# Attention and expert kernel on one core: four early loads issued by ScalarE, and the order planned with other numbers

## The chip, the cores and the metric

The kernel runs on one core of one Trainium2 chip. The metric is the device time of one execution in microseconds (us), the median of several runs.

## The reference

The reference is attention with rotary positions, followed by a two-layer expert with a leaky activation. Batch 4, 8 heads, sequence 576, head size 64; model width 512, hidden width 2048.

```python
q_rot, k_rot = (rotate(q), rotate(k))          # x1*cos - x2*sin, x1*sin + x2*cos
scores = scale * np.matmul(q_rot, k_rot.transpose(0, 1, 3, 2))
scores = scores - np.max(scores, axis=-1, keepdims=True)
attn = np.exp(scores)
attn = attn / (np.sum(attn, axis=-1, keepdims=True) + 1e-09)
out = np.matmul(attn, v)                        # (4, 8, 576, 64) -> x: (2304, 512)
h = x @ w_in
g = np.maximum(h, 0.0) + alpha * np.minimum(h, 0.0)
y = g @ w_out
```

All inputs are f32; w_in and w_out come as the words of 8-byte values, which VectorE puts together as f32.

## The kernel before

**Tiles and blocks.** The 2304 rows are 18 tiles of 128 rows, two to a block, so 9 blocks. A tile's attention goes by pairs of heads: queries and keys are loaded with a half-turned copy beside them, multiplied with the table of cosines and sines (`q_mul` L725, `k_mul` L516), and the two halves are added (`q_add` L733, `k_add` L525). TensorE makes the scores of two heads (L777), VectorE the maximum of each row (`mx`, L830), ScalarE the exponential and its sum (`exp`, L834).

**Two ways through.** In tiles 0 and 1 the exponentials stay in f32: TensorE turns them (`f_turn`, L874), ScalarE or VectorE copies them to SBUF (`f_copy`, L883 and L884), and TensorE multiplies with V (`f_pv`, L878). From tile 2 on they are split into a high and a low 16-bit part (`p_hi`, `p_lo`), a DMA transpose issued by SP turns them (`p_turn`, L851, tile `pt`), and TensorE multiplies (`pv`, L858). The experts are the same in f32 for blocks 0 and 1 (L945, L974) and in split 16-bit parts for the others (L951, L992). Weights come from DRAM into `wraw` buffers (L620); VectorE puts them together (L602, L607, L611), ScalarE takes their bound (L635, L645).

**What sets the order.** The program first writes a list of operations with their reads, writes and the engines that could run each. A planner (class `Plan`) then plays the list through, and each engine's instructions are issued in the order that it finds. For every engine that is free, it takes the waiting operation with the lowest due time. A due time is the operation's place (`at`, in units of 1/16 of a block) plus a number from the table `OFF`, by name and block or batch; the second engine that could run it adds a number from `PEN`. An operation with two possible engines goes to the one that is free and comes to it first. A load is planned on SP with 450 ns of issue, 1050 ns of delay and its size at 400 bytes per ns, behind the transfers planned before it; a DMA transpose has 1310 and 70 ns. For TensorE the planner keeps a book on the clock: every operation fills time with a weight `full`, and durations double while the book says that the clock is low. So every number in the tables can change the order on all engines, and none changes what is computed.

**The start.** On SP stand the two halves of the table (`tab`), `alpha`, tile 0's queries in two loads (`q_load`), the unit matrix (`eye`), and pair 0's and pair 1's keys in two loads each (`k_load`), then tile 1's queries and the values. All of these go through the helper `load`, L462 and L463. With `LEADS[0] = 3.15`, block 0's first pair has the place -19.15; a next pair of block 0 lies 2 later, tile 1's first pair 8 later. `tab` has -100, `alpha` -60, `eye` -59.

```python
keys:    load("k_load", b, at, r, ...)          # at: place of the pair
queries: load("q_load", t, at, raw, ...)        # at: place of the tile's first pair
run:     at = o.at + off(o.name, o.ph) + (pen(o.name, o.ph) if n else 0.0)
```

Of the kernel before, what the change touches and what calls it, by code (L numbers as in the profile page):

```python
# [45 lines left out]
    "a_bound": [13.39],  # L46
    "alpha": [4.11],
    "beta": [19.29],
    "eps": [-20.32],
    "exp": [-203.03, -13.08, -31.0, 7.42, -20.79, -6.72, -8.0, 2.63, 7.03],  # L50
    "eye": [20.48],
    "f_copy": [12.93],
    "f_pv": [14.63],
    "f_turn": [59.59],
    "gh": [-119.2, -119.2, -0.01, 27.77, -4.93, -6.46, 15.98, 77.17, 37.16],
    "gl": [329.17, 329.17, 3.75, 117.32, 59.74, -18.86, 34.4, 47.73, 66.05],
    "k_add": [15.8, -47.1, -62.28, 47.21],
# [12 lines left out]
    "pv": [-4.69, 13.78, 4.19, 3.85, 52.85, 0.63, -24.67, -14.01, 3.0],  # L70
    "q_add": [-9.89, -9.05, -13.47, -3.57, 13.4, 64.02, 22.21, -52.45, 79.61, 5.48, 28.34, 41.15, 10.07, 17.29, 0.89, 43.95, -3.57, 12.45],
    "q_hi": [126.19, 126.19, 126.19, 126.19, 126.19, -40.04, 20.21, -64.76, 17.73, 12.18, 7.82, 14.08, 21.0, -80.01, 13.39, -11.81, -24.61, -2.03],
    "q_lo": [-274.45, -274.45, -274.45, -274.45, -274.45, -5.86, -46.35, 2.77, 2.98, -5.57, 6.91, 31.12, 81.93, 51.48, -30.41, 5.61, -53.97, 18.63],
    "q_load": [-36.37, 13.88, -35.2, 9.7, -28.6, -11.73, -8.87, -103.41, 2.72, 9.37, -12.59, -11.1, -4.78, -14.91, -14.97, -8.7, -22.17, -23.39],
    "q_mul": [0.2, 30.31, 38.86, 32.22, 23.45, -6.9, 11.63, 40.42, 35.74, 16.54, 5.05, -21.77, -62.23, -14.81, -8.77, -21.73, 11.08, 110.02],
    "qd_hi": [151.43, 151.43, 82.32, 188.91, 235.61, 196.33, 29.99],
    "qd_lo": [8.59, 8.59, 20.78, -28.98, 85.57, 37.05, 4.13],
    "qd_zero": [-26.0, -26.0, 14.21, 88.92, 81.33, 26.3, 1.39],
    "relu": [-62.53, -48.77, -15.14, -35.39, -40.71, -80.66, -6.1, -1.65, 59.45],
    "res": [-79.62, -68.8, -29.62, -71.23, 62.15, 37.72, -40.93, -1.3, -1.64],  # L80
    "scores": [-34.62, 18.22, -3.17, -1.13, 2.75, 2.96, -29.27, -29.27, -0.88],
    "store": [-23.0, -149.27, -35.86, 55.49, 23.16, -23.49, 20.05, 10.42, -13.25],
    "tab": [-72.81, -3.78],
    "v_bound": [-8.18, 13.64, 68.86, -0.72],
    "v_hi": [0.49, -14.0, 43.8, 56.91],
# [16 lines left out]
    "wo_load": [55.26, 4.66, 16.03, 31.9],
    "x_hi": [-226.3, -226.3, 1.25, 16.57, -33.84, -50.05, -39.14, -24.72, 30.89],
    "x_lo": [113.28, 113.28, 23.69, -16.73, -45.15, -15.99, -85.91, 51.43, 0.18],
    "x_turn": [-86.07, -86.07, -0.04, 8.63, 97.54, 24.21, -20.71, 45.23, 34.62],
    "xw": [30.4, 30.4, 6.35, -56.71, -60.57, -24.46, -2.94],
    "y": [-35.54, 8.31, 67.96, -16.15, 14.03, -14.1, -10.06, -15.84, -90.05],
    "y_copy": [-2.21, 1.09],
    "y_turn": [42.78, 15.85],
# [1047 lines left out]
```

## Time and profile before

| | |
|---|---|
| median of 3 runs | 639.58 us (638.41 to 640.85) |
| the profiled execution | 643.7 us, span from first to last instruction 641.9 us |
| mean granted TensorE clock | 0.986 |
| VectorE, ScalarE, GpSimd busy | 76%, 56%, 34% of the span |
| the 16 DMA engines busy | 65.4% of the span by the main queue |
| moved | 90.97 MB, mean 142 GB/s |

Shares are of the span. The granted clock is 1.00 at full speed (2.4 GHz) and 0.5 at half (1.2 GHz); a mean over a stretch can lie between them. DMA share is the mean busy share of the 16 DMA engines. Engines in the rows: PE is TensorE's matmul, PEld its weight load, DVE VectorE, ACT ScalarE, POOL GpSimd, SPq the queue of SP.

### The profile page before, as it was taken

The page shows a single profiled execution, that of the slowest core. Times are in us where ns is not written, and L with a number is a line of the kernel's source. Part 1 is how long each engine was busy: PE and PEld are TensorE (multiplying, and loading weights), DVE is VectorE, ACT ScalarE, POOL GpSimd, SP SyncE. Part 2 cuts the span into 40 slices and gives each one's busy share as a digit, 9 for nine tenths or more (in the row PEclk, how much of TensorE's full clock was granted, in tenths as well). Part 3 has the DMA queues.
Part 4 walks back from the last instruction along what each step waited for, and adds up shares of the span by engine and source line. Part 5 has one row for each costly group of instructions (what it writes and reads, how often), then busy time and mean ns, then how long its engine had stood idle before and what let it go on. Part 6 is the DMA issues. An engine that isn't in the chain of part 4 may idle for free.

```text
span 641.9 us, 13987 instructions
## 1 busy us (share of the span) xinstructions
PE 602.4 (94%) x5478; PEld 431.1 (67%) x5478; DVE 485.0 (76%) x800; ACT 360.7 (56%) x808; POOL 218.5 (34%) x178
## 2 busy tenths in 40 slices
PE   1789789999999999999998999999999999999997
PEld 1668656667776767677665777777777667776664
DVE  5797979999999876769986789879985537853332
ACT  1455756555795648547665566767653435733332
POOL 4470300016746516436633343585331101210000
PEclk9878999999999999999999999999999999999999
DMA  8951798958955659759898977976855303752000
GB/s 303 407 178 64 240 275 211 261 79 202 215 130 111 121 88 173 133 92 198 146 187 140 165 145 108 189 129 161 129 111 92 87 1 66 135 103 24 34 1 34
DMA packets 188499, 90.97 MB, mean 142 GB/s; under 512 B 168721, under 2 KB 176529, under 8 KB 188433
## 3 DMA queue, kind: packets, MB, share of 16 engines
q1 hardware_dynamic: 188432, 90.08, 65.4%
q8 instruction: 43, 0.70, 0.5%
q14 instruction: 24, 0.19, 0.1%
HBM read 41.82 MB, written 4.72 MB: 72 GB/s over the span
## 4 chain that ended last, share of the span: by engine, by line
PE 68%; DMA 17%; DVE 9%; ACT 2%; issue 2%; SPq 1%; POOL 0%; DVEq 0%; ACTq 0%; POOLq 0%
PE h L951 20%; PE pair L992 20%; PE pair L777 8%; PE v L858 7%; DMA pt<-pp 7%; PE h L945 5%; DMA wraw<-in_moe_w_in_dram 5%; PE pair L974 4%; DVE mx L830 2%; DMA wraw<-in_moe_w_out_dram 2%; DVE pp L847 1%; PE pair L874 1%; PE v L878 1%; DVE r L968 1%; DMA kraw<-in_k_dram 1%
## 5 line engine op out<-in xcount | busy, mean ns | idle before, releaser
L951 PE MATMUL h<-xt,wi 128*128 128x256 f16 (+1 forms) x1344 | 165.2, 273 | 2.1 <-DVE r L968 1.2
L951 PEld LDWEIGHTS <-wi 128*128 128x128 f16 (+1 forms) x1344 | 129.3, 98 | 37.0 <-issue 5.2
L992 PE MATMUL pair<-wh,gh 128*128 128x512 f16 x448 | 133.4, 379 | 0.3 <-DVE os L470 0.3
L968 DVE SCALAR_TENSOR_TENSOR r<-r,beta,h 128x256 f32<-128x256 f32 x144 | 68.5, 476 | 64.8 <-ACT r L965 63.1
L830 DVE TENSOR_REDUCE mx<-pair 128x1 f32<-128x576 f32 x144 | 103.1, 749 | 12.3 <-PE pair L777 8.7
L965 ACT ACTIVATE r<-h 128x256 f32<-128x256 f32 x144 | 54.7, 380 | 101.0 <-PE h L951 69.8
L834 ACT ACTIVATE e<-pair,mx 128x576 f32<-128x576 f32 x112 | 82.2, 737 | 43.5 <-DVE mx L830 42.7
L985 POOL TENSOR_TENSOR gl<-r,gh 128x256 bf16<-128x256 f32 x57 | 51.1, 897 | 133.4 <-ACT gh L982 116.0
L847 DVE SCALAR_TENSOR_TENSOR pp<-e,pp 128x576 f16<-128x576 f32 x96 | 82.8, 870 | 8.6 <-ACT pp L843 7.6
L858 PEld LDWEIGHTS <-pt 128*128 128x128 f16 (+1 forms) x2016 | 71.6, 101 | 23.8 <-DMA pt<-pp 10.9
L992 PE MATMUL pair<-wh,gl 128*128 128x512 f16 x224 | 84.9, 379 | 0.0
L858 PE MATMUL v<-vv,pt 128*128 128x64 f16 (+1 forms) x2016 | 78.5, 194 | 6.7 <-DMA pt<-pp 6.6
L982 ACT ACTIVATE gh<-r 128x256 f16<-128x256 f32 x106 | 43.7, 414 | 47.8 <-PE pair L992 29.2
L945 PE MATMUL h<-xt,wi 128*128 128x256 f32 x256 | 61.8, 384 | 4.5 <-DVE r L968 3.5
L974 PE MATMUL pair<-wo,r 128*128 128x512 f32 x128 | 61.9, 607 | 0.0
L945 PEld LDWEIGHTS h<-xt,wi 128*128 128x128 f32 x256 | 47.5, 190 | 21.2 <-DVE r L968 7.8
L992 PEld LDWEIGHTS <-gh 128*128 128x128 f16 x448 | 39.9, 98 | 32.1 <-issue 2.1
L777 PE MATMUL pair<-kh,qn 64*128 64x288 f32 x576 | 50.9, 308 | 0.0
L985 DVE TENSOR_TENSOR gl<-r,gh 128x256 bf16<-128x256 f32 x55 | 27.4, 499 | 27.3 <-ACT gh L982 27.2
L777 PEld LDWEIGHTS pair<-kh,qn 64*128 64x128 f32 x576 | 39.7, 184 | 11.0 <-issue 7.8
L843 ACT ACTIVATE pp<-e 128x576 f16<-128x576 f32 x59 | 40.1, 680 | 8.7 <-DMA pt<-pp 7.0
L725 POOL TENSOR_TENSOR qr<-qr,tab 128x1024 f32<-128x1024 f32 (+1 forms) x14 | 29.4, 2106 | 34.6 <-DMA qr<-in_q_dram 34.6
(124 smaller groups left out, 755.5 us busy)
## 6 DMA issues: line engine op xcount, KB each, us to landing
qr<-in_q_dram SPq DMA_DIRECT2D x17, 512.0 KB, 4.8
wraw<-in_moe_w_in_dram SPq DMA_DIRECT2D x16, 512.0 KB, 5.8
wraw<-in_moe_w_out_dram SPq DMA_DIRECT2D x16, 512.0 KB, 6.7
kraw<-in_k_dram SPq DMA_DIRECT2D x12, 576.0 KB, 4.8
out_dram<-os SPq DMA_DIRECT2D x18, 256.0 KB, 2.2
vraw<-in_v_dram SPq DMA_DIRECT2D x12, 320.0 KB, 3.8
kraw<-in_k_dram SPq DMA_DIRECT2D x8, 288.0 KB, 7.1
vv<-vv SPq DMA_DIRECT2D x32, 64.0 KB, 2.5
```

Source lines behind the costliest of these rows:

```text
L777: nc.tensor.matmul(out=ps[h]()[:, x, :HS], lhsT=qn()[r, p] if b == 0 else qn()[r, i, p], rhs=kt()[r, c] if b == 0 else kt()[r, j, c], star ...
L830: lambda e: nc.vector.tensor_reduce(out=mx()[a:z], in_=ps()[a:z, :, :HS], axis=AX.XY, op=ALU.max, negate=True),
L834: lambda e: nc.scalar.activation(out=e_y() if t in IN_PLACE else e_y().rearrange("p (x c) -> p x c", x=2), in_=ps()[a:z, :, :HS], func=ACT ...
L847: lambda e: nc.vector.scalar_tensor_tensor(out=e_z(pp()[a:z, 1]), in0=e_y(), scalar=E_SC, in1=e_z(pp()[a:z, 0]), op0=ALU.mult, op1=ALU.sub ...
L858: nc.tensor.matmul(out=v_b()[c:d, 2 * p + g], lhsT=pt()[:, s, o:o + d - c], rhs=vt()[:, g, w], start=(n == 0), stop=(n == len(order) - 1))
L945: nc.tensor.matmul(out=h_y(), lhsT=w32(kk, j // FG)[:, f], rhs=x()[:, kk], start=(kk == 0), stop=(kk == KC - 1))
L951: nc.tensor.matmul(out=h_y(), lhsT=wt.bitcast(BF16) if w else wt, rhs=xs.bitcast(BF16) if y else xs, start=(kk == 0 and n == 0), stop=(kk ...
L965: lambda e: nc.scalar.activation(out=g(), in_=h_y(), func=ACTF.Relu, scale=-1.0),
L968: lambda e: nc.vector.scalar_tensor_tensor(out=g(), in0=g(), scalar=beta_b()[:, j:j + 1], in1=h_y(), op0=ALU.mult, op1=ALU.add),
L974: nc.tensor.matmul(out=po()[:, x], lhsT=g()[:, x * 128:(x + 1) * 128], rhs=wf[j // 2]()[:, j % 2], start=(j == 0), stop=(j == KF - 1))
L985: lambda e: ENG[e].tensor_tensor(out=gl(), in0=g(), in1=gh(), op=ALU.subtract),
L992: nc.tensor.matmul(out=po()[:, x], lhsT=s()[:, ts], rhs=w, start=(j == 0 and c == 0), stop=(j == KF - 1 and c == 2))
```

## The change

Three things change. First, `load` gets an argument `first`; with it the load is issued by ScalarE and planned with 480 ns on that engine. It is given for tile 0's queries, `alpha` and `eye`. Second, the planner's model: all engines start at 800 ns, a DMA transpose that finds more than 200 ns of transfers queued ahead of it takes 800 ns more of the transfer time, and the weights `full` of five operations in the book on the clock are other numbers. Third, all numbers of `OFF` and `PEN` (some 500) and three constants are new.

```diff
-    "k_add": [15.8, -47.1, -62.28, 47.21],
+    "k_add": [11.07, -14.72, -13.74, 12.24],
-    "k_load": [-0.18, -49.98, -22.1, 11.87],
+    "k_load": [-31.77, -8.33, -4.32, -64.95],
-    "alpha": [4.11],
+    "alpha": [1.56],
-    "eye": [20.48],
+    "eye": [-0.94],
-    "q_load": [-36.37, 13.88, -35.2, 9.7, ...
+    "q_load": [1.15, -28.05, -24.01, 9.81, ...
-    "tab": [-72.81, -3.78],
+    "tab": [-27.28, -23.21],
-    "v_load": [30.89, -20.13, 4.99, 11.68],
+    "v_load": [-9.8, -11.66, -37.11, -9.65],
...
 PEN = {
-    "k_add": [6.07, -5.88, 33.15, -22.07],
+    "k_add": [9.48, -88.82, -8.62, -1.45],
...
-PW, LW, BACKLOG = 174.78, 6.46, 4989.5
+PW, LW, BACKLOG = 53.71, 21.81, 4657.9
...
     def run(self):
-        free = [0.0] * 5
+        free = [800.0] * 5
...
-        events = [0.0]
+        events = [800.0]
...
                     if e == SP:
                         issue, lag, moved = dur
+                        if lag < 100 and dma > t + issue + lag + 200:
+                            moved += 800
                         dma = max(dma, t + issue + lag) + moved
...
-    def load(name, ph, at, buf, size, dst, src, writes=None):
-        op(name, ph, at, {SP: dma(size)}, lambda e: nc.sync.dma_start(out=dst(), in_=src), writes=writes or [buf])
+    def load(name, ph, at, buf, size, dst, src, writes=None, first=None):
+
+        op(name, ph, at, {ACT: (480, first)} if first else {SP: dma(size)},
+           lambda e: ENG[e].dma_start(out=dst(), in_=src), writes=writes or [buf])
...
             load("q_load", t, at, raw, 128 * 4 * len(xs) * 128 * 4, lambda c=c: raw()[:, :, c], q[t][:, :, c],
-                 writes=[(raw, (p[2], x)) for p in parts for x in xs])
+                 writes=[(raw, (p[2], x)) for p in parts for x in xs], first=4000 if t == 0 else None)
...
-        op("scores", i, at, {PE: mm(1080 if b == 0 else 986)}, scores, kind=ROWS, full=0.8,
+        op("scores", i, at, {PE: mm(1080 if b == 0 else 986)}, scores, kind=ROWS, full=0.89 if b == 0 else 0.73,
...
-        op("f_turn", i, at + 0.3, {PE: mm(550)}, turn, reads=[ex, eye_b], writes=[ps], full=0.6)
+        op("f_turn", i, at + 0.3, {PE: mm(550)}, turn, reads=[ex, eye_b], writes=[ps], full=0.97)
...
-            op("f_pv", i, at + 0.6, {PE: mm(1130)}, lambda e, g=g, o=o: pv(e, g, o), reads=[pt, raw], writes=[(v_b, (2 * p + g, c))], full=0.9)
+            op("f_pv", i, at + 0.6, {PE: mm(1130)}, lambda e, g=g, o=o: pv(e, g, o), reads=[pt, raw], writes=[(v_b, (2 * p + g, c))], full=0.47)
...
-            op("y_turn", i, at, {PE: mm(440)}, turn, reads=[(y, a), eye_b], writes=[(vo, (h, a)) for h in range(H)], full=0.6)
+            op("y_turn", i, at, {PE: mm(440)}, turn, reads=[(y, a), eye_b], writes=[(vo, (h, a)) for h in range(H)], full=0.97)
...
-    load("alpha", 0, -60, alpha_b, 8192, alpha_b, alpha)
-    load("eye", 0, -59, eye_b, 128 * 512, eye_b, eye)
+    load("alpha", 0, -60, alpha_b, 8192, alpha_b, alpha, first=5000)
+    load("eye", 0, -59, eye_b, 128 * 512, eye_b, eye, first=5000)
```

## Rows read from the trace of the kernel before

**Rows 1.** The page: busy us of each engine, share of the span, instructions.
```profile
PE 602.4 (94%) x5478; PEld 431.1 (67%) x5478; DVE 485.0 (76%) x800; ACT 360.7 (56%) x808; POOL 218.5 (34%) x178
```

**Rows 2.** Busy time by stage: stretch, length, busy us by engine, clock, DMA share, GB/s.
```profile
0.00:14.39 14.39, 0.56 (x3) 0.51 (x3) 6.66 (x15) 1.65 (x2) 6.28 (x11) 1.00 0.85 290
14.39:40.82 26.43, 20.55 (x123) 16.18 (x123) 22.50 (x26) 14.63 (x32) 16.06 (x8) 0.92 0.82 319
40.82:54.00 13.18, 13.18 (x57) 10.66 (x57) 8.39 (x10) 5.04 (x10) 5.99 (x5) 0.51 0.37 126
72.00:100.00 28.00, 22.98 (x129) 14.62 (x128) 23.74 (x31) 16.68 (x38) 3.63 (x2) 1.00 1.03 265
100.00:638.00 538.00, 528.48 (x5045) 374.29 (x5041) 406.00 (x694) 308.94 (x703) 185.22 (x153) 1.00 0.65 123
```

**Rows 3.** TensorE's waits on pt: us, times, longest; whole span, then 300 to 350.
```profile
PE v L858 <- DMA pt<-pp: 6.6, 9, 2.4
...
PE v L858 <- DMA pt<-pp: 3.9, 4, 2.4
```

**Rows 4.** Timeline, all engines, 0 to 30 us: start, us, instruction, idle before it.
```profile
0.74 1.28 ACT L550 ACT_TABLE_LOAD   x1 [0.74 <-PEq L1143]
1.68 0.42 SPq L463 DMA_DIRECT2D alpha<-in_moe_alpha_dram  x1
2.14 1.34 SPq L463 DMA_DIRECT2D qr<-in_q_dram  x2
4.17 1.85 SPq L463 DMA_DIRECT2D kraw<-in_k_dram  x4
6.20 1.29 DVE L725 TENSOR_TENSOR qr<-qr,tab 128x512 f32<-128x512 f32 x2 [0.96 <-DMA qr<-in_q_dram]
7.53 0.83 DVE L733 TENSOR_TENSOR qp<-qr 128x256 f32<-128x256 f32 x1
10.28 0.82 DVE L516 TENSOR_TENSOR kraw<-kraw,tab 128x576 f32<-128x576 f32 x1 [1.13 <-DMA kraw<-in_k_dram]
12.42 4.25 POOL L525 TENSOR_TENSOR ks<-kraw 128x576 f32<-128x576 f32 x2
14.02 0.74 ACT L550 ACTIVATE junk<-vraw 128x640 bf16<-128x640 f32 x1 [12.00 <-DMA vraw<-in_v_dram]
14.39 2.29 PE L777 MATMUL pair<-ks,qp 64*128 64x288 f32 x8 [5.44 <-POOL ks L525]
```

**Rows 5.** DMA view, 0 to 40 us: GB/s in 40 slices of 1 us.
```profile
GB/s 0 25 249 332 193 331 250 264 364 362 403 411 412 418 414 422 402 414 410 406 394 406 391 396 414 413 414 401 410 416 416 396 419 251 51 16 0 0 29 225
```

**Rows 6.** Tile kraw, 0 to 30 us: durations in ns and landing, min/median/max.
```profile
L525 POOL TENSOR_TENSOR ks<-kraw x3: 1912/2252/2380, 12.4 to 27.9; 128x576 f32<-128x576 f32 x3
L525 DVE TENSOR_TENSOR ks<-kraw x1: 759/759/759, 24.4 to 24.4; 128x576 f32<-128x576 f32 x1
...
DMA to landing us min/median/max: 4.8/7.7/8.6
```

**Rows 7.** Timeline of TensorE, 14 to 100 us.
```profile
36.80 2.44 PE L878 MATMUL v<-vraw,pt 128*128 128x64 f32 x20
40.82 2.39 PE L874 MATMUL pair<-eye,e 128*128 128x128 f32 x10 [1.57 <-ACT e L834]
...
45.36 4.53 PE L878 MATMUL v<-vraw,pt 128*128 128x64 f32 x20
```

**Rows 8.** Busy time of two more stretches, as in rows 2.
```profile
48.00:60.00 12.00, 11.32 (x69) 9.55 (x68) 8.17 (x9) 5.20 (x10) 1.41 (x2) 0.76 0.01 2
100.00:140.00 40.00, 39.42 (x272) 25.90 (x269) 38.70 (x59) 21.83 (x48) 0.83 (x4) 1.00 0.84 195
```

**Rows 9.** Timeline of SP's queue, 300 to 350 us.
```profile
308.14 5.78 SPq L851 DMA_TRANSPOSE pt<-pp  x2
...
337.71 13.48 SPq L851 DMA_TRANSPOSE pt<-pp  x4
```

**Rows 10.** The chain of waits that ended last, 60 to 100 us: start, us, what.
```profile
87.47 6.80 DMA wraw<-in_moe_w_in_dram
```

More of the change, by code (lines that the diff above doesn't have):

```diff
@@ L70 @@
[L70 to L73, printed above, removed]
@@ L102 @@
[L102 to L109, printed above, removed]
+    "a_bound": [-9.02],
@@ new lines @@
+    "alpha": [1.56],
+    "beta": [17.73],
+    "eps": [-0.6],
+    "exp": [55.08, -0.64, -10.43, 11.35, 5.79, -5.23, 4.6, -3.46, 4.66],
+    "eye": [-0.94],
+    "f_copy": [-3.36],
+    "f_pv": [23.99],
+    "f_turn": [-16.03],
+    "gh": [-14.94, -14.94, 28.31, 4.92, 2.89, -12.24, 28.66, 22.04, 8.67],
+    "gl": [-38.91, -38.91, -70.02, -26.51, 0.7, 40.23, 4.53, -3.6, 8.22],
+    "k_add": [11.07, -14.72, -13.74, 12.24],
+    "k_hi": [169.23, -27.16, 4.09, 35.13],
+    "k_lo": [138.46, 18.94, 9.47, 47.19],
@@ new lines @@
+    "k_load": [-31.77, -8.33, -4.32, -64.95],
+    "k_mul": [17.31, 4.2, 13.47, 9.43],
[3 rows of a table added]
+    "norm": [15.97, 33.91, 5.19, 51.9, -22.77, 7.62, -19.5, 1.51, -3.93],
+    "p_hi": [187.67, -1.07, 33.92, -47.4, 1.18, -8.35, 1.59, -15.57, -3.78],
+    "p_lo": [-70.55, -98.52, -70.56, 2.7, -54.7, 1.45, 0.0, -6.11, -0.97],
+    "p_turn": [-340.94, -61.66, 12.95, -6.45, -35.2, -6.03, -20.27, 0.01, 4.08],
+    "prelu": [-102.73, -104.84, -70.45, -146.48, -32.04, -40.46, -12.21, -18.81, 4.18],
+    "pv": [25.38, 2.51, 12.68, 20.64, -23.41, 5.17, 44.37, 1.65, 23.69],
@@ new lines @@
+    "scores": [14.35, -19.14, -22.11, -1.48, -1.97, 19.28, -35.63, -1.17, -25.28],
+    "store": [-38.64, -10.7, -15.0, 16.47, 4.71, 18.17, -74.05, -3.88, -29.91],
+    "tab": [-27.28, -23.21],
+    "v_bound": [19.42, -17.79, 23.81, 12.8],
+    "v_hi": [95.53, 9.01, 12.21, -27.08],
+    "v_lo": [1.91, -8.96, -55.67, 10.65],
+    "v_load": [-9.8, -11.66, -37.11, -9.65],
+    "v_max": [3.66, 27.45, 1.3, -39.3],
+    "v_shift": [-7.28, 77.34, -66.52, 12.28],
+    "wi_abs": [-22.08, -4.94, -9.23, 24.16],
@@ new lines @@
+    "wi_bound": [-19.95],
+    "wi_conv": [13.46, -16.41, -7.85, -45.63],
+    "wi_hi": [7.71, 0.43, 88.38, 1.96],
+    "wi_lo": [22.61, 14.98, 15.76, 7.71],
+    "wi_load": [-20.64, 8.71, 57.63, 22.86],
+    "wi_scale": [-8.27, -7.78, 33.13, 44.22],
+    "wo_abs": [3.88, 39.59, -55.69, -24.57],
+    "wo_bound": [-4.05],
+    "wo_conv": [12.62, 10.87, 31.09, -8.32],
+    "wo_hi": [61.47, -13.49, -31.46, -14.25],
+    "wo_lo": [-16.02, -7.01, 1.37, 15.59],
+    "wo_load": [-33.84, 0.7, 4.4, 52.14],
@@ L110 @@
+    "x_hi": [142.66, 142.66, 28.21, -19.72, 8.94, 56.1, 101.81, -42.33, -2.04],
+    "x_lo": [-226.76, -226.76, -57.29, -57.21, -7.63, -29.71, 8.73, 26.28, 1.46],
+    "x_turn": [31.03, 31.03, -18.87, -27.18, 58.18, 6.37, -18.59, 43.14, 80.21],
+    "xw": [-86.84, -86.84, 29.27, -9.81, 1.13, -142.31, -25.93],
+    "y": [-21.02, -4.77, -25.37, -31.66, -20.67, -7.36, 20.58, -17.82, -99.49],
+    "y_copy": [9.25, 23.12],
+    "y_turn": [3.54, -11.18],
 }
 PEN = {
-    "a_bound": [26.53],
-    "eps": [-47.85],
@@ new lines @@
+    "q_mul": [218.04, 202.56, 170.46, 194.05, 153.78, 250.85, 199.09, 158.31, 163.63, 125.65, 161.52, 185.3, 175.95, 157.31, 224.69, 225.12, 200.18, 213.47],
+    "qd_hi": [-54.79, -54.79, 18.81, -51.08, -41.58, -133.21, 7.14],
+    "qd_lo": [60.32, 60.32, 23.39, 150.42, 219.14, 148.64, 35.74],
+    "qd_zero": [21.06, 21.06, -8.63, 98.18, 77.5, 50.13, -2.94],
+    "res": [39.31, 16.71, 41.5, 33.04, 43.73, 10.18, 50.92, 48.15, 51.38],
+    "v_bound": [0.04, -7.81, 1.12, 44.08],
+    "v_max": [-42.56, 67.56, 3.16, 18.91],
@@ L141 @@
+    "wi_bound": [37.46],
+    "wi_hi": [16.85, -6.07, 23.07, 1.84],
+    "wi_lo": [42.78, 11.0, 23.11, 2.12],
+    "wi_scale": [1.23, -22.22, -7.7, -17.29],
+    "wo_bound": [-1.57],
+    "wo_hi": [-198.35, 21.62, 18.42, 5.97],
+    "x_hi": [60.26, 60.26, 16.31, 86.67, -83.74, 0.11, -34.27, 48.06, 30.58],
+    "x_lo": [217.38, 217.38, 23.19, 5.98, 32.29, 14.51, 28.89, 27.52, 45.28],
+    "y_copy": [-22.7, -83.24],
 }
-PW, LW, BACKLOG = 174.78, 6.46, 4989.5
+PW, LW, BACKLOG = 53.71, 21.81, 4657.9
```

91 lines of the change are left out of this document (22 added, 69 removed), and 6 rows, old and new, of the table OFF.

## The prediction

> **What bounds the kernel now.** I read the profile from coarse to fine. First the page [rows 1]: TensorE is busy 602.4 us of a span of 641.9 us, VectorE 485.0, ScalarE 360.7. So TensorE sets the end, and time can only come from two places: the 39.5 us in which it is idle, and work that it does at the lower of its two clocks.
>
> Then busy time by stage [rows 2]; idle is the length less TensorE's busy time. TensorE is idle 13.83 us before the first scores at 14.39, 5.88 in 14.39 to 40.82, none in 40.82 to 54, 5.02 in 72 to 100, and 9.52 in the 538 us from 100 to 638. What is left of the 39.5, 5.2 us, lies in 54 to 72 and behind the last matmul. The row 40.82 to 54 has no idle time, but a granted clock of 0.51: TensorE ran at 1.2 GHz instead of 2.4. So the first 100 us hold 24.7 us of idle time and the slow clock; in five times that length behind them little is left.
>
> Third, who TensorE waited for [rows 3]: 6.6 us for transposes that SP issues (pt), 3.9 of them in 300 to 350.
>
> **Part 1: four loads leave SP's queue.** In the first 6 us SP issues one load after another [rows 4]: two of tab, alpha at 1.68, two of tile 0's queries from 2.14, eye at 3.52, and only then four halves of keys from 4.17. Alpha, queries and eye go to ScalarE. By the new due times (a load's place plus its OFF) SP then has tab (-127 and -123), pair 0's keys (-19.15 - 31.77 = -50.9), pair 1's keys (-48.9), tile 1's queries (-39.2), then values (-29.0). So pair 0's keys go out where alpha stood, 4.17 - 1.68 = 2.49 us earlier, and what is behind them moves up with them. ScalarE issues eye (-59.9), alpha (-58.4), then the two query loads: four issues at SP's 0.42 us (alpha) to 0.67 (half of 1.34, the queries) are about 2 us. Its activation table load takes 1.28 us at 0.74, and its first operation runs at 14.02 [rows 4]; about 3.3 us of new work in a gap of 12 cost nothing. If the table load stays ahead of the issues, the first query load goes out at 0.74 + 1.28 + 2 x 0.43 = 2.9 us instead of 2.14. That is no loss while the keys are last, as they are now: in the trace the queries are in use at 6.20, the second half of pair 0's keys at 10.28.
>
> How much of the 2.49 us arrives is set by bandwidth. Summing the row by 1 us slices [rows 5], some 1640 KB had moved by 8 us, 2008 by 9 and 2370 by 10 (slices of 1 us in GB/s). Tab, alpha, the queries, eye and pair 0's keys are 1736 KiB, 1.78 million bytes, moved by some 8.4 us; but pair 0's second half came into use only at 10.28, when pair 1's bytes (2.37 million in all) had moved too: loads in flight share the engines and land almost together. The slices from 2 to 8 us average 270 GB/s, the next three 376. Two issuers can fill the first ones; 2.37 million bytes from 2 us at 363 GB/s (the slice from 9) land at 8.5. I take 1.5 us; the ends are 0 and 2.49.
>
> The Trainium skill (DMA: Bandwidth & Descriptors, Issuing engines are not separate DMA queues) says that loads started from several engines run on the same transfer engines and interleave, and that one saves only the issuing sequencer's time by it. The rows agree: from 10 to 32 us the slices stay between 391 and 422 GB/s, whatever is queued [rows 5]. By the rule alone the landing could gain 2.49 us at most; by the bytes it gains 1.5.
>
> Behind the landing stands a choice of engine. VectorE finished pair 0's second product at about 11.10, but the sum of the two halves ran on GpSimd, behind pair 1's product, from 12.42 to about 14.35 [rows 4]. The same sum on VectorE took 0.76 us against 1.91 to 2.38 [rows 6]. A plan that sums at once on VectorE would save 1.32 of queue and about 1.2 of duration, 2.5 us. The terms don't settle the engine (before, due -3.35 on GpSimd and 2.72 on VectorE; after, -8.1 and 1.4): either takes it when free. I take half, 1.3. The start: -2.8 us, ends 0 and -5.0.
>
> **Part 2: the clock's terms.** The planner keeps a book on TensorE's clock, in which each operation counts with a weight `full`: attention with V in f32 (f_pv) falls from 0.9 to 0.47, the turns of the exponentials rise from 0.6 to 0.97, scores from 0.8 to 0.89. The trace is on the side of the new weights. The clock fell after 20 f_pv matmuls at 36.80 and an idle 1.57 us, at 40.82, and stayed at half through 13 us of gapless work that held another f_pv group of 4.53 us [rows 7, 8]. A plan that counts f_pv at 0.9 is not likely to foresee it. What the stretch costs: 13.18 us at 0.51 are 6.5 us lost; the 20 f_pv matmuls at 45.36 took 4.53 us against 2.44 for those at 36.80, about the same factor. In 14.39 to 40.82 the granted clock is 0.92 [rows 2], another 2.1. VectorE was 4.8 us idle of 13.18 in the slow stretch, and the transfer engines nearly idle from 48 to 60 [rows 2, 8]: both waited for TensorE there, so that a faster TensorE is not at once stopped by them. But from 72 to 100 the transfer engines are full (1.03) and TensorE is idle 5.02 us, so part of what comes in early waits there. Of 8.6 us I take 3.5. Ends: -8.6, and +6.5 if the new order has one more such stretch.
>
> **Part 3: the transfers' terms.** A DMA transpose that finds more than 0.2 us of transfers queued is now charged 0.8 us more, and the clock of the plan begins at 800 ns, as SP does at 0.74 us. This moves no work; it lets the planner see waits like those of 300 to 350, where SP's row shows two transposes in 5.78 us and four in 13.48 [rows 9], some 3 us each. Of the 6.6 us of waits on pt I take 2.0 back; ends -6.6, and +3.9 (a second stage like 300 to 350).
>
> **Part 4: everything else is re-ordered.** All due times are new numbers. The amount of work is the same: the same matmuls, copies and bytes. What a fresh order costs is waits that its planner doesn't see. The order of before has up to 9.5 us of these after 100 us [rows 2], and a new order will have its own; I add +1.0 for places that get worse (ends 0 and +5).
>
> **Sum.** -2.8 - 3.5 - 2.0 + 1.0 = -7.3 us on a span of 641.9. The profiled execution took 643.7 us, 1.8 more than its span, and is 4.1 us above the median of the runs, 639.58. I take the difference off the median: 632.3 us.
>
> **Rivals.**
> B, the gains are swallowed: the start is earlier, but the stage 72 to 100, full of transfers (1.03), takes it back. For it: the chain of waits runs there over a load of w_in of 6.80 us [rows 10]. Against: the transfer engines were free from 48 to 60, so loads can also move up. Then only part 3 and half of part 2 remain, less new waits of 3: -2.0 - 1.75 + 3 = -0.75, 638.8 us.
> C, slower: weight loads give way to transposes. SP issues both from one queue, and charging a transpose for queued transfers makes it pay for the planner to hold loads until transposes are out. If the loads of w_in and w_out slip, TensorE stands through 72 to 140, where transfers take 1.03 and 0.84 of the time [rows 2, 8], as it now does in 72 to 100: 18% of 68 us are 12.2 us, against 5.02 + 0.58 now; the start's gain is lost behind it. +6.6, less part 3's 2.0, plus 1 of new waits: 645.2 us. It decides as soon as loads of weights end last in more of 60 to 140 us than now. Against: these loads carry due times of their own, and from 14 to 54 us much of the transfer time is free (shares 0.82 and 0.37).
> D, all of it comes: -5.0 - 8.6 - 4 = -17.6, less what 72 to 100 holds back (3): 625.0 us. For it: before 100 us 24.7 us of idle time and 8.6 of slow clock stand open. Against: the same amount of VectorE work, 22.5 of 26.43 us in the stage that releases the scores [rows 2].
> E, ScalarE's loads don't help: queries that share the engines with keys, pair 1, tile 1 and values land later than the keys. Even at the slowest landing of keys, 8.6 us [rows 6], from 2.9, they land at 11.5, and half of 1.29 of product and 0.83 of sum follow [rows 4]: scores at 13.0, still before 14.39. The start then gives 1.4, and the sum -5.9: 633.7, inside the forecast.
>
> **Chances.** The forecast (E in it) 0.54, with its own range 627 to 636.3; B 0.21; C 0.17; D 0.08. A measurement of this kernel tells about 0.5%, 3.2 us, from no change. Faster by more: forecast and D, 0.62 less 0.02 for its edge, 0.60; within: B and that edge, 0.23; slower: C, 0.17. Range 624.5 to 643.5: it leaves out most of C and the better half of D.
>
> **What would show it.** The first scores should start at 11 to 13 us instead of 14.39, keys issued by SP third and fourth, and four issues on ScalarE before 5 us. The granted clock should have no stretch of 13 us at 0.5; if one is there, part 2 fails. Waits on pt should fall below 4.6 us, and those of 300 to 350 below 2. TensorE's idle time in 72 to 140 tells B and C: about 5.6 or less for the forecast, above 9 for C. The prediction is wrong if the busy time of TensorE does not fall by some 3 us, or if idle time after 100 us is above 14.

## The result, and the profile after

The changed kernel is slower. Its median is 642.65 us (20 runs, 639.76 to 652.42), that of the kernel before beside it 639.31 us (20 runs, 635.5 to 643.77); the ratio is 1.0059, 95% interval 1.0033 to 1.0085. I had forecast 632.3 us. Ratios, here and below, leave out the runs of either kernel that lie over 1.5% above its fastest, while medians and ranges are of all runs, so that a ratio is not the quotient of the medians beside it.

The profile taken with this result fell on the longest of its runs (652.42 us, mean clock 0.982). The rows here are therefore from a repeat of the same kernel, n2_after_again, whose profiled execution took 645.11 us, span 643.3. The kernel before was profiled a second time too (n1_before_again, 639.79 us).

Busy time by engine, to set against [rows 1]:

```profile
PE 604.2 (94%) x5478; PEld 429.1 (67%) x5478; DVE 488.9 (76%) x803; ACT 366.0 (57%) x813; POOL 218.4 (34%) x170
```

TensorE's busy time rose by 1.8 us, where I had said that it must fall by 3; VectorE's rose by 3.9 for three instructions more. Next the windows, with the columns of [rows 2]. To the stretches shown there I add three: up to the first expert matmul (71.9 us here), from there to the last matmul, and the first 60 us of block 2's expert.

```profile
0.00:71.90 71.90, 52.34 (x324) 43.32 (x324) 51.57 (x74) 36.04 (x72) 39.27 (x26) 0.95 0.62 230
...
72.00:100.00 28.00, 24.14 (x145) 15.60 (x146) 24.41 (x32) 18.05 (x41) 1.01 (x3) 1.00 1.01 261
100.00:638.00 538.00, 526.87 (x5008) 369.97 (x5007) 412.06 (x698) 311.09 (x701) 178.00 (x143) 1.00 0.61 124
...
71.91:638.75 566.84, 551.85 (x5154) 385.79 (x5154) 436.56 (x730) 329.23 (x741) 179.10 (x145) 1.00 0.63 130
...
237.00:297.00 60.00, 56.95 (x605) 40.56 (x605) 51.33 (x72) 38.87 (x89) 34.52 (x26) 1.00 0.77 150
```

The added stretches of the kernel before, from its own trace:

```profile
0.00:74.90 74.90, 53.04 (x325) 43.42 (x325) 56.65 (x79) 37.45 (x73) 31.88 (x24) 0.89 0.65 238
...
74.88:637.34 562.46, 549.43 (x5154) 387.67 (x5154) 427.63 (x721) 322.55 (x735) 186.60 (x155) 1.00 0.66 129
...
240.00:300.00 60.00, 58.79 (x598) 41.83 (x599) 43.84 (x69) 38.36 (x87) 30.57 (x24) 1.00 0.78 146
```

Read them in pairs. The start is 3.0 us shorter (74.88 to 71.91). The rest holds the same 5154 matmuls in both kernels and is 4.4 us longer (562.46 to 566.84): 2.0 us of it idle time (13.03 to 14.99), 2.4 busy time. In block 2's first 60 us TensorE was idle 1.21 us before and is idle 3.05 now, while VectorE is busy 51.33 us with 72 instructions instead of 43.84 with 69. So some 1.8 of the 4.4 us are idle time there; what the experiments make of it comes below.

TensorE's waits over the whole span, to set against [rows 3]:

```profile
PE v L862 <- DMA pt<-pp: 4.5, 8, 1.2
PE h L955 <- DVE r L972: 3.8, 4, 1.9
```

Those on pt went from 6.6 to 4.5 us, and in 300 to 350 from 3.9 to this:

```profile
PE v L862 <- DMA pt<-pp: 0.3, 2, 0.2
```

But the kernel before, unchanged, has in its second profile, over the whole span and then in 300 to 350:

```profile
PE v L858 <- DMA pt<-pp: 3.8, 7, 0.8
...
PE v L858 <- DMA pt<-pp: 1.0, 2, 0.8
```

So waits on pt differ as much between two profiles of one kernel, and their fall cannot be put down to the change. The waits for r are another matter: 3.8 us now, in the first profile of before

```profile
PE h L951 <- DVE r L968: 1.2, 2, 0.8
```

and 0.9 in its second. Here r is the output of the leaky activation; VectorE's operation on it reads h, whose one buffer the split experts' next matmuls write. The start, all engines, against [rows 4]:

```profile
1.67 3.25 SPq L467 DMA_DIRECT2D kraw<-in_k_dram  x4
1.68 1.27 ACTq L467 DMA_DIRECT2D qr<-in_q_dram  x2
2.98 1.28 ACT L554 ACT_TABLE_LOAD   x1 [2.98 <-issue]
...
7.89 0.76 DVE L520 TENSOR_TENSOR kraw<-kraw,tab 128x576 f32<-128x576 f32 x1 [1.41 <-DMA kraw<-in_k_dram]
8.15 3.43 POOL L729 TENSOR_TENSOR qr<-qr,tab 128x512 f32<-128x512 f32 x2 [7.28 <-DMA qr<-in_q_dram]
...
11.54 2.43 POOL L737 TENSOR_TENSOR qp<-qr 128x256 f32<-128x256 f32 x2
...
12.83 2.29 PE L781 MATMUL pair<-ks,qp 64*128 64x288 f32 x8 [12.83 <-POOL qp L737]
```

The four loads go out on ScalarE ahead of its table load, and SP issues the keys at 1.67 us instead of 4.17. Pair 0's second product on VectorE starts at 7.89 instead of 10.28. But the queries are in use at 8.15 instead of 6.20, their products and sums run on GpSimd, and the scores wait for the queries' sum instead of the keys'. TensorE then, against [rows 7]:

```profile
17.05 2.40 PE L878 MATMUL pair<-eye,e 128*128 128x128 f32 x10 [1.42 <-ACT e L838]
19.38 2.29 PE L781 MATMUL pair<-ks,qp 64*128 64x288 f32 x8
21.59 4.53 PE L882 MATMUL v<-vraw,pt 128*128 128x64 f32 x20
25.91 2.34 PE L878 MATMUL pair<-eye,e 128*128 128x128 f32 x10
28.18 2.10 PE L781 MATMUL pair<-ks,qp 64*128 64x288 f32 x8
30.21 2.44 PE L882 MATMUL v<-vraw,pt 128*128 128x64 f32 x20
...
40.07 2.32 PE L878 MATMUL pair<-eye,e 128*128 128x128 f32 x10 [2.46 <-ACT e L838]
...
53.99 2.40 PE L878 MATMUL pair<-eye,e 128*128 128x128 f32 x10 [1.15 <-ACT e L838]
```

The 13 us at half clock from 40.82 are gone in this profile. In their place stand 13 us of gapless work at half speed from 17.05 to 30.2, with the first f_pv group in them (4.53 us; 2.44 at 23.20 before). Durations tell it, twice those of the same groups later; the column of the granted clock reads 1.00 there. Two idle pieces, of 2.46 and 1.15 us, are each followed by a turn of twice its time (2.32 and 2.40 against 1.26). In the profile taken with the result, the second of them opens a stretch like that of before:

```profile
54.84:68.11 13.27, 13.27 (x56) 10.62 (x56) 5.48 (x7) 6.13 (x12) 0.00 (x0) 0.51 0.22 80
```

### The profile page after: what moved, and what is told of

It is laid out like the page before. It is cut to its first block, busy times and chain, and to the rows that moved or that the text cites. A ratio compares the mean times of both kernels' runs of the same rounds, so it can differ in the third digit from the quotient of the medians.

```text
span 650.6 us, 14023 instructions
## 1 busy us (share of the span) xinstructions
PE 610.2 (94%) x5478; PEld 433.6 (67%) x5478; DVE 488.7 (75%) x803; ACT 366.3 (56%) x813; POOL 219.4 (34%) x170
## 4 chain that ended last, share of the span: by engine, by line
PE 75%; DMA 12%; DVE 6%; issue 3%; ACT 3%; SPq 0%; ACTq 0%; DVEq 0%
PE pair L996 20%; PE h L955 19%; PE v L862 8%; PE h L949 8%; PE pair L781 8%; DMA pt<-pp 7%; PE pair L978 7%; PE pair L802 2%; PE pair L878 2%; DMA wraw<-in_moe_w_in_dram 2%; PE v L882 2%; DMA qr<-in_q_dram 1%; DVE pp L851 1%; DMA vraw<-in_v_dram 1%; DMA xt<-xs 1%
## 5 line engine op out<-in xcount | busy, mean ns | idle before, releaser
L955 PE MATMUL h<-xt,wi 128*128 128x256 f16 (+1 forms) x1344 | 166.9, 273 | 4.8 <-DVE r L972 3.5
L989 POOL TENSOR_TENSOR gl<-r,gh 128x256 bf16<-128x256 f32 x53 | 45.8, 864 | 169.2 <-ACT gh L986 103.2
L851 DVE SCALAR_TENSOR_TENSOR pp<-e,pp 128x576 f16<-128x576 f32 x96 | 87.6, 918 | 13.3 <-ACT pp L847 12.4
L986 ACT ACTIVATE gh<-r 128x256 f16<-128x256 f32 x100 | 41.3, 413 | 44.4 <-PE pair L996 33.9
L989 DVE TENSOR_TENSOR gl<-r,gh 128x256 bf16<-128x256 f32 x59 | 32.7, 555 | 25.8 <-ACT gh L986 25.4
L729 POOL TENSOR_TENSOR qr<-qr,tab 128x1024 f32<-128x1024 f32 (+1 forms) x19 | 43.7, 2305 | 21.8 <-DMA qr<-in_q_dram 21.8
L847 ACT ACTIVATE pp<-e 128x576 f16<-128x576 f32 x61 | 41.5, 680 | 14.2 <-DMA pt<-pp 8.2
```

What stands on the lines that cost most here:

```text
L851: lambda e: nc.vector.scalar_tensor_tensor(out=e_z(pp()[a:z, 1]), in0=e_y(), scalar=E_SC, in1=e_z(pp()[a:z, 0]), op0=ALU.mult, op1=ALU.sub ...
L955: nc.tensor.matmul(out=h_y(), lhsT=wt.bitcast(BF16) if w else wt, rhs=xs.bitcast(BF16) if y else xs, start=(kk == 0 and n == 0), stop=(kk ...
L989: lambda e: ENG[e].tensor_tensor(out=gl(), in0=g(), in1=gh(), op=ALU.subtract),
```

## The experiments

Ratios are to the kernel before on the same chip. "Stretch" is the time from the first expert matmul to the last matmul, 5154 matmuls in every kernel: 562.5 us for before's profile, 568.9 for the profile with the result, 566.8 for the repeat of after. A stretch is of one execution; a ratio is of all that were kept.

**Both kernels again.**

> The kernel before, unchanged, for the spread of its span with the granted clock. Theory C (the clock): spans go with the mean clock; at a clock of 0.995 and above some 634 to 636 us, at 0.986 the 642 of the profile, so that the median run had lost only part of the slow stretch which the prediction wanted to win back. Rival (the slow stretch is in every run): the clock stays between 0.984 and 0.988 in all runs, and the spread has another cause.

640.46 us, ratio 1.0034 (0.9998 to 1.0069), stretch 559.3. So one and the same kernel can stand 0.3% and 3.1 us of stretch from itself: a ratio of that size says nothing alone. Its runs go with the clock as theory C has it, and the rival's one clock in all runs did not come.

> The changed kernel, unchanged. Theory O (the order): at an undisturbed clock (0.995 and above) it spans 638 to 641 us, some 4 us more than the kernel before at the same clock, and its profile has more idle time of TensorE after 72 us than the 14.5 of before. Theory C alone: at the same mean clock both kernels span the same within 1.5 us, and it is slower only because its clock falls more often.

641.77 us, ratio 1.0062 (1.0030 to 1.0093). The loss repeats. The clock is loose in both: of the 29 runs of before beside this one, those at a mean clock of 0.994 or more average 637.2 us (18 runs), those below 0.99 641.2 (7). The repeat's runs at 0.994 or more average 641.1 us (7 runs). So at a like clock the changed kernel takes 3.9 us more, as theory O has it: the order loses, and the clock alone does not explain it.

**The loads alone.** In before's order the four loads go to ScalarE; in after's they go back to SP.

```diff
-    lambda e: nc.sync.dma_start(...)          # before
+    lambda e: ENG[ACT].dma_start(...)         # e1: tile 0's queries, alpha, eye
-    lambda e: ENG[e].dma_start(...)           # after
+    lambda e: nc.sync.dma_start(...)          # e2: all loads
```

> The order of before, engine by engine, with alpha, tile 0's queries and eye issued by ScalarE instead of SP and nothing else changed. Prediction, part 1: keys in use 1.5 us earlier, first scores at about 12.9 instead of 14.4, and up to 1.5 us less in all. Theory Q (the queries share the transfer engines with the keys and land last): queries in use at 8 to 9 us instead of 6.2, first scores between 13.5 and 15, and the time within 0.2% of before.

637.38 us, ratio 0.9987 (0.9954 to 1.0020): no difference, and the first scores start at 14.58 us, both as theory Q has it.

> The order of after, engine by engine, with the four loads issued by SP among the others (eye, tab, alpha, then keys and queries in turn). If the loads on ScalarE do the harm: 3 us faster than after. If the order does it (theory O): within 1.5 us of after, scores starting 0.5 to 2 us later than 13.65, because the last keys and queries are issued up to 2 us later.

649.39 us, ratio 1.0128 (1.0076 to 1.0179), of 6 runs. The loads on ScalarE are not what after's order loses by. Neither theory had this much more: the first scores start at 13.27 us, not late, and the stretch is 570.6 us. Why it is so slow stays open.

**Spliced orders.** The planner's loop is replaced by a list of the operations in the order in which it had issued them, each with the engine that it had chosen, so that order and engines of one kernel can be followed up to an operation and those of the other from there on. All but s2 have the four loads on ScalarE; s2 begins as before does, with all loads on SP.

```diff
-        while left: ...                       # the planner
+        for k, e in zip(ORDER[0::2], ORDER[1::2]):
+            self.ops[k].fn(e)
```

> The first 229 operations in the order of after (everything before its first expert, with the four loads on ScalarE), all others in the order of before. Theory O (the new order loses behind the first expert, not before it): from the first expert to the end some 566 us as in before, against 571 to 574 in after, and the time 636 to 639. Rival S (the new start, with its clock at half from 13 to 30 us, is what costs): 641 us or more, as after.

642.56 us, ratio 1.0043 (1.0001 to 1.0086). The seam, at the first expert, made a wait of its own, 6.5 us for r at 78.71, so that this run decides little.

> The reverse: the first 236 operations in the order of before (loads on SP), all others in the order of after. Theory O: 642 to 646 us, 571 us or more behind the first expert. Rival S: 637 to 640 us.

647.65 us, ratio 1.0135 (1.0086 to 1.0184). Before's start with after's order behind it has the largest ratio of all. That puts the loss behind the start, but it is more than theory O named, and what the seam adds is not known.

> The order of after for 900 operations, up to the first expert of block 2 at about 238 us, then the order of before. Tells where behind the first expert the loss is. TensorE's idle time from 72 to 240 us was 6.6 and 4.7 in two profiles of before, 6.4 and 5.7 in two of after; from 240 on 8.0 and 5.0 against 9.7 and 9.3. So theory O late: 637 to 640 us, most of the loss gone. Theory O early: 641 us or more.

637.02 us, ratio 0.9981 (0.9945 to 1.0018), stretch 562.2. With before's order and engines from block 2's first expert on, no loss is left that can be told. The windows of this kernel, block 2's first 60 us and the stretch:

```profile
233.00:293.00 60.00, 59.03 (x598) 41.89 (x599) 44.34 (x73) 40.29 (x92) 32.07 (x25) 1.00 0.74 144
...
66.52:628.69 562.17, 550.91 (x5154) 386.65 (x5154) 429.15 (x719) 331.44 (x750) 180.67 (x148) 1.00 0.64 132
```

TensorE is idle 0.97 us in the 60, and VectorE does 73 instructions in 44.34 us. Its waits from 240 us on:

```profile
PE v L751 <- DMA pt<-pp: 3.6, 8, 0.9
PE h L844 <- DVE r L861: 1.0, 2, 0.6
```

**The seam at block 3 and at block 5.**

> The order of after up to block 3's first expert operation, the order of before from there on. Measure: the time from the first expert matmul to the last matmul, for 5154 matmuls in every kernel here; so far 559.3 to 563.0 with the order of before behind the start or behind block 2's first expert, 565.9 to 570.6 with the order of after. Theory L (the loss is made by VectorE's long pieces beside GpSimd's in block 2, 281 to 289 us, where TensorE waits 1.86 and 1.05 us for r): this kernel has the whole loss, 566 to 568 us, and a ratio of 1.004 to 1.006. Rival S (every block of the new order has some such waits, 1 to 2 us a block): 563 to 564.5 and a ratio near 1.000, as s3.

640.87 us, ratio 1.0041 (1.0008 to 1.0075), stretch 567.0.

> The order of after up to block 5's first expert operation, the order of before from there on. Theory L: as s4_after_to_block3, within 1 us, 566 to 568. Rival S: 2 to 3 us more than s4_after_to_block3, 565.5 to 567. If the loss is made behind block 5 alone, both kernels stay at 562 and at a ratio of 0.998.

641.49 us, ratio 1.0052 (1.0022 to 1.0083), stretch 569.5. With block 2 in after's order the loss is back: stretch and ratio of the first kernel are what theory L named. The second lies 2.4 us further in the stretch, which S named and L did not, but only 0.9 above the first kernel's own repeat (568.6, below); the ratios don't tell the two kernels apart. So whether blocks 3 and 4 add anything is open.

**What block 2 does.** VectorE in the repeat of after, then GpSimd, then TensorE, as timelines:

```profile
278.21 0.68 DVE L904 SCALAR_TENSOR_TENSOR y<-v,rs 128x512 f32<-128x512 f32 x1
278.81 2.58 DVE L851 SCALAR_TENSOR_TENSOR pp<-e,pp 128x576 f16<-128x576 f32 x1
281.31 0.47 DVE L972 SCALAR_TENSOR_TENSOR r<-r,beta,h 128x256 f32<-128x256 f32 x1
...
285.22 2.85 DVE L989 TENSOR_TENSOR gl<-r,gh 128x256 bf16<-128x256 f32 x1
287.99 0.47 DVE L972 SCALAR_TENSOR_TENSOR r<-r,beta,h 128x256 f32<-128x256 f32 x1
...
292.07 0.42 DVE L989 TENSOR_TENSOR gl<-r,gh 128x256 bf16<-128x256 f32 x1
```

```profile
277.96 2.81 POOL L520 TENSOR_TENSOR kraw<-kraw,tab 128x1152 f32<-128x1152 f32 x1
...
284.64 3.14 POOL L520 TENSOR_TENSOR kraw<-kraw,tab 128x1152 f32<-128x1152 f32 x1
```

```profile
281.83 1.47 PE L955 MATMUL h<-xt,wi 128*128 128x256 f16 x12 [1.86 <-DVE r L972]
...
288.51 1.47 PE L955 MATMUL h<-xt,wi 128*128 128x256 f16 x12 [1.04 <-DVE r L972]
```

While GpSimd multiplies keys, one pp takes 2.58 us and one gl 2.85, and each ends just behind the product: pp at 281.39 (the product at 280.77), gl at 288.07 (287.78). With GpSimd idle gl takes 0.42 in the same fence, and s3's pp takes this:

```profile
277.22 0.76 DVE L740 SCALAR_TENSOR_TENSOR pp<-e,pp 128x576 f16<-128x576 f32 x1
277.89 0.48 DVE L861 SCALAR_TENSOR_TENSOR r<-r,beta,h 128x256 f32<-128x256 f32 x1
```

Both times r stands behind the stretched operation, and TensorE behind r. The two orders also choose engines differently here: from 225 to 330 us all four products of keys stand on GpSimd in s4_again (below), two of them on VectorE in s3.

Two swaps on VectorE put r ahead of the one, and the gl behind the next r:

```diff
-  ... p_lo (pp) ... r 920 ...  gl 929 ... r 934 ...
+  ... r 920, p_lo (pp) ...  r 934, gl 929 ...
```

> After, its order kept but for two neighbours on VectorE in block 2: a prelu (r) is put ahead of a p_lo (pp), and a gl behind a prelu. In the profiles of after TensorE waits there 1.86 and 1.05 us for r, each time while VectorE's pp or gl takes 2.6 to 2.9 us instead of 0.8 and 0.4 beside a product of keys of 2.8 to 3.1 us on GpSimd. Theory P (VectorE's work is held up beside GpSimd's, and the new order puts such work in front of what TensorE waits for): both waits go, the stretch from the first expert of block 2 to the end falls from 405.7 to 407.8 us to 403 to 405, the median by 2 to 3 us, to about 639.5. Rival N (TensorE's waits only move on, the next stage is late instead): waits of the same sum show up within 20 us behind them, and stretch and median stay within 1 us of after.

640.17 us, ratio 1.0024 (0.9989 to 1.0060), stretch 565.9, waits for r from 240 us on 1.8 us instead of 3.8. The direction is as theory P has it, but the stretch is within 1 us of after's repeat, as rival N has it, and the intervals of this kernel and of after overlap. So the same swaps were made in s4, beside a repeat of it.

> The same kernel as s4_after_to_block3, beside the next one on one chip. Expected: 640 to 642 us, r waits behind 240 us of some 4.3 us, from the first expert matmul to the last matmul 566 to 568.

642.60 us, ratio 1.0041 (1.0006 to 1.0077), stretch 568.6.

> s4_after_to_block3 with the two swaps of t1_two_swaps on VectorE in block 2: r ahead of one of p_lo's operations, and one of gl's behind r. Theory P (block 2 loses because r stands on VectorE behind operations that GpSimd's products stretch from under 1 us to over 2.5): the waits for r behind 240 us fall from 4.3 to some 2, the stretch from the first expert matmul to the last falls from 567 to 564 to 565, and the median lies 2 to 3 us below s4_again. Rival Q (the waits move to another tile, as VectorE has the same work in the same 60 us): other waits take the place of r's, and the median lies within 1 us of s4_again.

644.36 us, ratio 1.0034 (0.9999 to 1.0069), stretch 564.2. TensorE's waits from 240 us on, first in s4_again, then in t2:

```profile
PE h L844 <- DVE r L861: 4.6, 4, 1.9
PE v L751 <- DMA pt<-pp: 3.8, 8, 1.1
```

```profile
PE v L751 <- DMA pt<-pp: 4.4, 7, 1.1
PE h L844 <- DVE r L861: 2.3, 3, 1.3
PE pair L670 <- ACT e L727: 0.7, 1, 0.7
```

And the windows, s4_again's stretch and block 2's first 60 us, then t2's 60 us:

```profile
66.06:634.68 568.62, 550.89 (x5154) 386.33 (x5154) 436.00 (x717) 330.38 (x749) 184.44 (x150) 1.00 0.63 130
...
234.00:294.00 60.00, 56.37 (x599) 40.14 (x600) 50.55 (x71) 38.02 (x87) 33.66 (x26) 1.00 0.79 151
```

```profile
232.00:292.00 60.00, 57.80 (x609) 41.07 (x608) 48.52 (x72) 39.06 (x89) 35.20 (x27) 1.00 0.77 149
```

The swaps halve the waits for r, and TensorE's idle time in the 60 us falls from 3.63 to 2.20; s3 has 0.97. But VectorE's operations are still stretched (48.52 us for 72 against 44.34 for 73), and pt and e take over 1.3 us of the wait. The gain is not resolved in the times: the median stands above s4_again's and the ratios are alike. P came in the profile (the waits, and a stretch of 564.2 us), not in the median, and Q holds in part. Both swaps move places in the order alone; no run gives the products of keys back to VectorE alone.

**Tile 0's queries on VectorE.**

```diff
-    lambda e, ...: ENG[e].tensor_tensor(            # q_mul, q_add
+    lambda e, ...: ENG[DVE if t == 0 else e].tensor_tensor(
```

> After, with the four products and sums of tile 0's queries on VectorE instead of GpSimd, in the same places of the order. Theory Q: queries land at about 8.5 to 9; products at 0.65 and sums at 0.4 us each on VectorE instead of 1.7 and 1.2 on GpSimd bring the first scores from 13.65 to 11 to 12. If the start sets the end (the prediction's part 1), the time falls by 1.5 us or more; if it is swallowed before the first expert, it stays within 1 us of after.

644.99 us, ratio 1.0051 (1.0008 to 1.0094). The first scores start at 12.29 us, the earliest of all orders, and the time does not follow in a way that can be told.

**TensorE kept busy in the start.** Extra matmuls, whose results go nowhere, stand in TensorE's idle gaps; f1 and f2_filled have s3's order, f2_after that of after.

```diff
+    def fill(to, n):
+        for _ in range(n):
+            nc.tensor.matmul(out=to, lhsT=tab_b()[:, 0, :128], rhs=tab_b()[:, 1, :256], ...)
```

> The order of s3 (after up to block 2, then before) with 19 extra f32 matmuls of 128x256 on the table of cosines, whose results nobody reads: 13 ahead of the first scores, and 3 each in two places where TensorE waited 1.4 and 1.25 us for exponentials (second pair of tile 0, first of tile 1). They use otherwise idle time. Theory C (the slow clock of the first 70 us costs what it lengthens): first scores and what follows run at full clock, the first expert starts at 62 to 64 us instead of 66.5 to 70, the spread towards longer runs goes, and the median falls by 2 to 4 us to 633 to 635. Rival W (VectorE and the loads set this stage): the matmuls run fast, but the first expert starts at 66 us or later and the median stays within 1 us of 637.

639.71 us, ratio 0.9962 (0.9920 to 1.0003). The first scores ran at full clock (eight in 1.24 us), but an idle piece of 2.61 us behind them was left, and the next f_pv was at half speed again; the first expert starts at 76.1 us. This run does not test theory C.

> The splice s3 (order of after up to block 2's first expert, the order of before from there on) with 26 extra matmuls, whose results are not used, in TensorE's idle gaps of the first 60 us: 13 ahead of the first scores, 6 ahead of the first f_turn, 3 ahead of pair 1's and 4 ahead of tile 1's f_turn. Theory C (what the start gains or loses is TensorE's clock): with no idle gap left TensorE stays at 2.4 GHz, the first expert starts at 61 to 64 us instead of 66 to 77, spans near 631 in nearly all runs, median about 633, below both kernels. Rival W (VectorE and the loads set the stage, or the clock falls elsewhere): first expert at 66 or later and a median of about 637, as s3 and before have it.

640.15 us, ratio 1.0020 (0.9992 to 1.0049). Every f_pv group up to the first expert runs at full speed (2.44 us), the turns at 1.26 to 1.49 us and the first scores at 1.80 for 1.24, yet the first expert starts at 66.3 us, as in s3 (66.5): theory C's 61 to 64 did not come. In the stage full of transfers the wait comes all the same, here for a transpose behind a load of values, and a half-speed group behind it (eight such matmuls take 1.89 at 99.40). The stretch, 567.1 us, is as long as after's, though before's order stands behind block 2: it is no measure of the order alone.

```profile
91.01 0.93 PE L751 MATMUL v<-vv,pt 128*128 128x64 f16 x14 [3.66 <-DMA pt<-pp]
91.75 3.76 PE L838 MATMUL h<-xt,wi 128*128 128x256 f32 x8
```

> The whole order of after with the same 26 extra matmuls as f2_filled. If the loss lies in the order from block 2's first expert on, whatever the clock did in the start, this is 5 to 6 us above f2_filled, with a last stage (first expert of block 2 to the end) of 405 to 408 us against 400 to 401. Rival (the loss comes from the clock that the start leaves behind): within 1.5 us of f2_filled.

642.12 us, ratio 1.0054 (1.0022 to 1.0086), stretch 567.5, the first expert at 65.8 us: a start nearly without half speed does not lift after's loss. It stands 2 us above f2_filled, between the two theories; it has the wait at 90 us as well (3.51 us for pt), and from block 2's first expert to the end it takes 405.3 us, as expected, but f2_filled 402.5 instead of 400 to 401. The pair decides less than it was meant to.

No version beats both kernels by more than the measurement tells: s3 lies at 0.998 of before, f1_filled at 0.996.

**All together.** Nine measurements have after's order and engines in block 2: after and its repeat, e2, e3, s2, s4 twice, s5 and f2_after. All nine intervals lie above 1, and in their profiles TensorE waits 3.3 to 5.6 us for r in the split experts. Six have those of before there: n1, e1, s1, s3, f1 and f2_filled. Only the interval of s1, with its 6.5 us at the seam, lies above 1, and TensorE waits 0.6 to 1.6 us for r. Waits on pt don't go with the order: 3.7 to 9.9 us in the six, 4.3 to 7.9 in the nine.

## Why the prediction was wrong

Set against the sum, the pair of profiles reads so: up to the first expert -3.0 us, where parts 1 and 2 had -6.3; behind it +4.4, where parts 3 and 4 had -1.0.

The step that failed is **part 4, "everything else is re-ordered"**: I added +1.0 us, with +5 as its end, for waits that the new plan doesn't see. The rest behind the first expert became 4.4 us longer in this pair, and 4.4 to 9.6 over the two profiles of each kernel (559.3 and 562.5 before, 566.8 and 568.9 after). I had looked for places in the trace of before where the new order would wait less, and priced by one guess what it would do to the 538 us behind 100 us. They are 84% of the time, and TensorE had 9.5 us of idle time in them to lose from and any amount to gain.

The place is block 2, as far as the runs tell: s3 and s4 differ by its order and engines alone, and their ratios are 0.998 and 1.004 (the latter twice; the intervals overlap by 0.001). What stands there in place of the +1.0 is TensorE's wait for r, 3.3 to 5.6 us where before's order has 0.6 to 1.6: VectorE's pp and gl are held up beside GpSimd's products, and r stands behind them. The stretches, 562.2 against 567.0 and 568.6 us, overstate it. Between s3 and s4_again TensorE's busy time is equal and its idle time is 11.3 and 17.7 us, but of these 6.5 us only 2.7 lie in block 2's first 60, 2.5 ahead of them, where both kernels have the same order, and 1.3 behind. In the 60 us VectorE takes 6 to 7 us longer for about as many instructions (44.34 us for 73 in s3, 50.55 for 71 in s4_again). They are not the same ones: products of keys have gone to GpSimd.

That the waits for r are all of the loss is not shown: taking half of them away moved no median that can be told apart. Nor is it shown whether the places in the order or the choice of engines makes them. The planner keeps a book on this too: its variable `port` lets such an operation of VectorE start when GpSimd's is done, and one that doesn't need the port go ahead of it if it is due within `PW`, which the change takes from 174.78 to 53.71. I did not price that, and no run changes it alone. The 2.4 us of busy time between the profiles of before and after stay open as well; the two profiles of before differ by 1.3 in it themselves.

**Part 3 is not shown**, though its number came: waits on pt fell by 2.1 us in 6.6 (I said 2.0), and both of its marks were met. The kernel before met them too, unchanged, in its second profile (3.8 us, 1.0 of them in 300 to 350), and e1, with its order, has 8.3. SP's transposes in 300 to 350 still stand two and three in a row in the repeat of after. So the agreement is luck, as far as these profiles tell.

**Part 1 went as rival E**, which I held inside the forecast. The keys came 2.4 us earlier and the queries 2 us later, and the sum on VectorE that I counted at half was the wrong sum: the queries' products and sums on GpSimd now end last. The scores start 1.6 us earlier in the repeat, 0.7 in the run with the result (13.65). The Trainium skill (DMA: Bandwidth & Descriptors, Issuing engines are not separate DMA queues) says that such loads interleave; the trace agrees, in that what one queue won the other lost. And in e3 even 12.29 brought nothing that can be told at the end.

**Part 2 was counted from one slow start, and by its own sign it failed.** A stretch of 13 us at half speed was to refute it, and there is one in either profile of after. Of the 8.6 us, 2.1 were read off the column of the clock, which reads 1.00 from 18.81 to 23, where a turn and scores took 2.40 and 2.13 us; so the column missed part of that loss. I took 3.5 of 8.6 us that the profiled execution had lost to half clock, and then also took off the 4.1 us by which it stood above the median: the same loss, in part twice. How much the start loses differs from run to run of one order. With after's order up to the first expert it begins that expert at 65.4 us in s5 and at 77.1 in the profile with the result; TensorE's 324 matmuls of the start take 56.39 us with the result, 52.34 in the repeat and 46.30 here, in s5:

```profile
0.00:65.40 65.40, 46.30 (x324) 38.12 (x324) 51.31 (x74) 36.30 (x72) 40.64 (x26) 1.00 0.68 251
```

So 53.04 (325) against 46.30 (324) prices half clock in before's profiled start at some 6.7 us, an estimate, and after's two lose 6.0 and 10.1 in their own way: the new order moved the slow pieces and removed none that the median shows. What the weights did in it no run tells apart from the rest.

**The rivals.** C had the sign and, at 645.2 us, nearly the size, by another mechanism: idle time in 72 to 100 fell from 5.02 to 3.86 us in the repeat, and in 72 to 140 it is 4.4 us there and 6.3 with the result, where C wanted above 9. B named a stage that swallows a better start; f2_filled and f2_after have a wait of over 3.5 us in it, but their first expert, at 66.3 and 65.8, starts hardly earlier than in s3 (66.5) or later than in s5 (65.4), so that B is not tested. Of my two marks of being wrong one tripped: TensorE's busy time did not fall by 3 us. The other mark, idle time behind 100 us above 14, did not trip (11.1), though that stage is what lost: a mark of idle time alone missed the busy time and the shift of work between stages.

## What to carry to other kernels

When an order is planned anew, price the long stage behind the edit first: list, for its fullest block, what stands on the second engine ahead of the operation that TensorE needs next, and bound the new waits by as much as that engine's longest operation beside its neighbour, not by the waits of the old order. Don't take a gain out of one profiled execution that stood above the median and then also subtract its distance from the median. Take a second profile of the unchanged kernel before a wait that fell is put down to the change. To find where two orders differ, splice them, and compare ratios of many runs first: stretches that hold the same number of matmuls differ by 3 us between two profiles of one kernel.

## What the runs showed of the hardware

VectorE's operations with both inputs in SBUF are stretched beside GpSimd's products: pp from 0.76 to 2.58 us, gl from 0.42 to 2.85. They end 0.62 and 0.29 us behind the product, and two other pp of block 2 (2.51 us at 271.75, 1.14 at 284.15) end 0.61 behind GpSimd's operation, so that the price goes by what is left of that operation and is no fixed factor. One with a single input in SBUF can be held up too, the high part of the exponentials (0.46 us at 262.29, with GpSimd idle):

```profile
246.22 2.46 DVE L474 TENSOR_SCALAR pp<-e 128x576 f16<-128x576 f32 x1
...
246.00 2.36 POOL L729 TENSOR_TENSOR qr<-qr,tab 128x1024 f32<-128x1024 f32 x1
```

One that reads its large input from PSUM is not: y takes 0.68 us at 278.21, inside the same product of GpSimd, and 683 ns in its mean over the blocks. The Trainium skill (GPSIMD Engine Reference, Specifications) says that the two engines share SBUF interfaces and that VectorE's operations with two SBUF inputs, or in a mode with two ports, contend; the trace agrees for the first kind, and gives the price, 1.8 and 2.4 us for these two operations. Whether the high part ran in such a mode no run here shows.

TensorE's clock differs between runs of one kernel on one core, from 0.982 to 1.00 in the mean, and some 4 us go with it here (637.2 against 641.2 us for before). In the first 100 us the groups behind idle pieces of 1.15 to 3.66 us took up to twice their time. In block 2 they did not: behind 1.86 us of idle time, at 281.83, twelve matmuls took 1.47 us, as they do without a gap.
